# One operand product per group, elementwise work off GpSimd, and projections split 9, 8, 7 in the second MLP of an attention kernel

## The chip, the core and the metric

The kernel runs on one core of a Trainium2 chip. TensorE (PE) multiplies matrices into PSUM; VectorE (DVE), ScalarE (ACT) and GpSimd (POOL) do elementwise work; SyncE (SP) issues every DMA. Each engine works through its own list of instructions strictly in order and waits for others by semaphores. The metric is device time in microseconds (us): 1600.27 us, the median of three runs (1599.98 to 1604.18).

## The reference

Three stages follow each other. A packed attention (8 batches, 8 heads, 576 positions, width 64) makes `x`, 4608 tokens of width 512. Then come two MLPs of width 2048 without biases:

```
h = x @ w_in;   x = (h * (1 / (1 + exp(-h)))) @ w_out      # first MLP
h = x @ w_in2;  out = (h * cos(h)) @ w_out2                # second MLP
```

Everything is float32; the MLP weights come as 64-bit floats, which the kernel decodes itself.

## The kernel before

A float32 product is made of three matmuls on pairs: a number is held as a rounded part and a rest, and rest by rounded, rounded by rest and rounded by rounded are summed in PSUM. `split` makes such a pair: one copy that rounds, one subtraction that leaves the rest.

**Two stages.** From about 0 to 800 us the attention and the first MLP run interleaved. Then comes the second MLP. Its 4608 tokens are cut into nine blocks of 2 x 256 tokens (`NBLK`), and for each block eight groups (`FH`) each take two of the sixteen 128-wide slices of the hidden layer: 72 groups in all.

**A group.** The first matrix product of a group (two token halves, two hidden slices, width 512 in two halves) is done as a 2 x 2 block product with seven products instead of eight. `multiply(s, k)` issues them in four parts, k = 0 to 3: products 0 and 1; 2 and 3; 4 and 5; 6. Between the parts the sums in PSUM are folded: after part 0 ScalarE copies `x1` into `hb` and `x2` into `gf`; after part 1 VectorE adds (`sb<-hb,gf` or `mb<-hb,gf`); after part 2 VectorE adds `hb<-hb,gf`. Part 2 of the products can't start before the first of these adds is done, and part 3 not before the second. In a profile a group is 42 matmuls of 256 columns (into `hb`, `mb`, `sb`) and 24 of 512 columns (into `acc`). `cosine` (ScalarE and VectorE, tiles `n`, `r`, `g`) follows parts 2 and 3, and `project`, two groups later, multiplies by `w_out2` into the four `acc` banks. `second(s)` sets the order: part 0, 12 projections, part 1, 6 projections, part 2, 6 projections, part 3.

**The operands of a block.** `load_y(i)` brings eight tiles `raw` (128 x 256) of the first MLP's output. Where the block holds tokens of the first pair of batches, three more partial sums (`ypart`) come for each tile through two buffers (`ysb`) and are added: 24 adds for blocks 3 and 4, 24 of 64 columns for block 5, none for the others. `put(prod)`, seven times, forms the operand pairs of one product for both halves of the width: up to two subtractions and two splits, into tiles that the profile calls `y`, `w` or `g` by the memory they use. Subtractions go through `combine`, which lets the planner choose VectorE or GpSimd; the rounding copies of `split` may be on ScalarE or VectorE.

**What sets the order.** Nothing is issued as the code stands. Every operation is recorded in a `Plan` with a cost; a list scheduler (`schedule`, `order`) then lists the instructions of all engines, eight rounds forward and backward over the whole kernel, and keeps the round with the earliest planned end. `plan.due` gives the latest times to aim at; in the second MLP a group is due every 10.48 us. From `plan.inorder = []` on, TensorE's operations keep the order of the code. The dependencies recorded in `record` decide the listing only: what an instruction waits for on the chip follows from the tiles it reads and writes. Since all are issued at one place, the profile gives one line (L207) to nearly all instructions, so they are told apart by their tiles.

Of the kernel before, what the change touches and what calls it, by code (L numbers as in the profile page):

```python
# [34 lines left out]
def f32(ap):  # L35

    return ap.bitcast(F32)


class Late:  # L40
# [3 lines left out]
    def __init__(self, key, ap, base=None, path=()):  # L44
        self.key, self.ap, self.base, self.path = key, ap, base or self, path
        if base is None:
            self.tile = None
# [32 lines left out]
class Plan:  # L80
# [21 lines left out]
    def __init__(self, nc):  # L102
        self.ops = []
        self.writes, self.reads = {}, {}
        self.due = None
        self.release = 0.0
        self.margin = 0
        self.inorder = None
        self.block = None
        self.choice = None  # L110
        self.V = self.Engine(self, self.DVE, nc.vector)
        self.A = self.Engine(self, self.ACT, nc.scalar)
        self.T = self.Engine(self, self.PE, nc.tensor)
        self.G = self.Engine(self, self.POOL, nc.gpsimd)
        self.D = self.Engine(self, self.DMA, nc.sync)
# [106 lines left out]
    def record(self, engine, emit, outs, ins, cost, issue):  # L222
        if self.block:
            op = self.ops[-1]
            assert op.engine == engine
            op.emit.append(emit)
            op.cost += cost
        else:
            op = Op()
            op.engine, op.emit, op.cost, op.issue, op.due = engine, [emit], cost, issue, self.due  # L230
            if self.block is not None:
                op.cost += self.TURN
            op.after, op.before, op.choice, op.sbuf = [], [], {}, False
            op.release = self.release
            op.margin = self.margin
            self.ops.append(op)
            if self.block is not None:
                self.block = True
        i = len(self.ops) - 1
        waits = set()  # L240
        if engine == self.PE and self.inorder is not None:
            waits.update(self.inorder)
            self.inorder = [i]
        for r in filter(None, ins):
            if r[1] is None:

                waits.update(
                    j
                    for _, j in self.reads.get(r[0], [])
                    if self.ops[j].engine != engine or self.ops[j].choice or self.choice is not None  # L250
                )
            waits.update(j for s, j in self.writes.get(r[0], []) if self.overlap(s, r[1]))
        for r in filter(None, outs):
            for d in (self.writes, self.reads):
                waits.update(j for s, j in d.get(r[0], []) if self.overlap(s, r[1]))
        for r in filter(None, outs):
            for d in (self.writes, self.reads):
                d[r[0]] = [(s, j) for s, j in d.get(r[0], []) if not self.covers(r[1], s)]
            self.writes[r[0]].append((r[1], i))
        for r in filter(None, ins):  # L260
            self.reads.setdefault(r[0], []).append((r[1], i))
        self.wait(op, i, waits)
# [140 lines left out]
def attention_mlps_kernel(  # L403
# [17 lines left out]
    P = 128  # L421
# [4 lines left out]
    FC = DFF // P  # L426
    KC = DM // P
    TB = 256
    NBLK = NT // (2 * TB)
    FH = FC // 2  # L430
# [4 lines left out]
    plan = Plan(nc)  # L435
# [4 lines left out]
    V, A, T, G, DMA = plan.V, plan.A, plan.T, plan.G, plan.D  # L440
# [43 lines left out]
    acc = [psum.tile([P, 512], F32, name=f"acc{i}") for i in range(4)]  # L484
# [18 lines left out]
    def change(stack, pools, name, side, new):  # L503


        def f():
            stack.close()
            pl = ctx.enter_context(pool(name, side, reuse_waits="tile"))
            for x in new:
                x.tile = pl.tile(list(x.ap.shape), x.ap.dtype, name=x.key)  # L510

        plan.switch(f, sum([cells[pl] for pl in pools], []), [x.key for x in new])
# [15 lines left out]
            V.tensor_copy(dst, src)  # L528

    def combine(dst, x, y, op):  # L530
        with plan.either():
            V.tensor_tensor(dst, x, y, op)
            G.tensor_tensor(dst, x, y, op)

    def split(d, x):

        copy(d[:, 0], x)
        combine(d[:, 1], x, f32(d[:, 0]), ALU.subtract)
# [399 lines left out]
    NS2 = NBLK * FH  # L938
    order = list(range(3, 6)) + [0, 1, 2] + list(range(6, NBLK))
    wout = {}  # L940
# [23 lines left out]
    def load_y(i):  # L964

        t0 = order[i] * TB
        n = min(TB, S - t0)

        def load(kc, h):
            st = raw()  # L970
            DMA.dma_start(st, ydram[kc, :, h * NT // 2 + t0 : h * NT // 2 + t0 + TB])
            for part in ypart if n > 0 else ():
                ad = yad()
                DMA.dma_start(ad[:, :n], part[kc, :, h * S + t0 : h * S + t0 + n])
                combine(st[:, :n], st[:, :n], ad[:, :n], ALU.add)
            return st

        b11 = [load(c, 0) for c in range(2)]
        b12 = [load(c, 1) for c in range(2)]
        b21 = [load(c + 2, 0) for c in range(2)]  # L980
        b22 = [load(c + 2, 1) for c in range(2)]
        t2 = [raw() for c in range(2)]

        def put(prod):
            for c in range(2):
                x, minus = {
                    0: (b11, None),
                    1: (b11, (b12, b11)),
                    2: (t2, (b22, b11)),
                    3: (b21, None),  # L990
                    4: (b12, (b22, b12)),
                    5: (b22, None),
                    6: (b21, (b21, t2)),
                }[prod]
                if minus:
                    combine(x[c], minus[0][c], minus[1][c], ALU.subtract)
                yt[i, prod, c] = yring()
                split(yt[i, prod, c], x[c])

        for prod in range(7):  # L1000
            put(prod)

    def load_wout2(c, w):
        wout[c] = w
        DMA.dma_start(f32(w), w2dram[c])
# [18 lines left out]
    def output(i, t):  # L1024

        o = oring()
        if t % 2:
            V.tensor_scalar(o, acc[t], WEIGHT**-2, None, op0=ALU.mult)
        else:
            A.activation(o, acc[t], AF.Copy, scale=WEIGHT**-2)  # L1030
        p0 = order[i] * TB + t % 2 * P
        cuts = [p0] + list(range(p0 // HALF * HALF + HALF, p0 + P, HALF)) + [p0 + P]
        for a, b in zip(cuts, cuts[1:]):
            r0 = a // HALF * S + t // 2 * HALF + a % HALF
            DMA.dma_start(out[r0 : r0 + b - a, :], o[a - p0 : b - p0])

    gt, st, m5s = {}, {}, {}

    def project(s, x, part):

        if not 0 <= s < NS2:
            return
        i, fp = divmod(s, FH)
        fc = fp + x * FH
        g, w = gt[s, x], wout[fc]
        if fc == FC - 1:
            passes = [(t, a, b) for t in range(4) for a, b in ((1, 0), (0, 1), (0, 0))]
        else:
            passes = [(t, 0, b) for b in (1, 0) for t in range(4)] + [(t, 1, 0) for t in range(4)]
        for n, (t, a, b) in list(enumerate(passes))[6 * part : 6 * part + 6]:  # L1050
            first = fc == 0 and n < 4
            last = fc == FC - 1 and n % 3 == 2
            T.matmul(acc[t], g[:, a, t * P : (t + 1) * P], w[:, b], start=first, stop=last)
            if last:
                output(i, t)

# [34 lines left out]
    def second(s):  # L1091

        plan.due = due_second(s)
        if s == 1:
            for k in range(4):
                for x in range(2):
                    multiply(x, k)
        elif s > 1:
            multiply(s, 0)
            project(s - 2, 0, 0)  # L1100
            project(s - 2, 0, 1)
            multiply(s, 1)
            project(s - 2, 1, 0)
            multiply(s, 2)
            project(s - 2, 1, 1)
            multiply(s, 3)
        plan.due = None

# [5 lines left out]
    def due_second(s):  # L1114
        return due_first(NS) + 10480 * s
# [70 lines left out]
    for pr in range(NPAIR):  # L1186
# [14 lines left out]
        for o in range(PAIR[pr + 1] - PAIR[pr]):  # L1201
# [7 lines left out]
            x = o - 48  # L1209
# [4 lines left out]

    change(top, [att], "yp", "right", raws + ys)
    change(mid, [a2p], "cp", "left", ns + rs_ + g2s + os_)
    load_y(0)
    plan.inorder = []
    for s in range(NS2 + 2):
        i, fp = divmod(s, FH)  # L1220
        if i == 0:
            for x in range(2):
                load_wout2(fp + x * FH, W[2 * fp + x])
        if fp == 0 and i + 1 < NBLK:
            load_y(i + 1)
        second(s)

    with tc.manual_schedule():
# [26 lines left out]
```

## Time and profile before

| | |
|---|---|
| median of 3 runs | 1600.27 us |
| profiled execution | 1597.47 us, span 1595.7 us |
| PE busy | 1544.8 us, 97% of the span |
| DVE busy | 1150.4 us, 72% |
| ACT busy | 780.6 us, 49% |
| POOL busy | 270.3 us, 17% |
| second MLP | about 800 us to the end |

A row of windows gives, for a stretch, the busy time and the count of instructions of each engine, TensorE's granted clock as a share, the busy share of the DMA engines and GB/s. A row of the timeline gives start, duration, engine, line, operation, tiles (out<-in), shapes, and in brackets the idle time before it and what ended it.

### The profile page before, as it was taken

The page shows a single profiled execution, that of the slowest core. Times are in us where ns is not written, and L with a number is a line of the kernel's source. Part 1 is how long each engine was busy: PE and PEld are TensorE (multiplying, and loading weights), DVE is VectorE, ACT ScalarE, POOL GpSimd, SP SyncE. Part 2 cuts the span into 40 slices and gives each one's busy share as a digit, 9 for nine tenths or more (in the row PEclk, how much of TensorE's full clock was granted, in tenths as well). Part 3 has the DMA queues.
Part 4 walks back from the last instruction along what each step waited for, and adds up shares of the span by engine and source line. Part 5 has one row for each costly group of instructions (what it writes and reads, how often), then busy time and mean ns, then how long its engine had stood idle before and what let it go on. Part 6 is the DMA issues. An engine that isn't in the chain of part 4 may idle for free.

```text
span 1595.7 us, 31482 instructions
## 1 busy us (share of the span) xinstructions
PE 1544.8 (97%) x11640; PEld 1384.5 (87%) x11640; DVE 1150.4 (72%) x2140; ACT 780.6 (49%) x1663; POOL 270.3 (17%) x294
## 2 busy tenths in 40 slices
PE   9989999999999999999999999999999999999999
PEld 7778888999789997999988888889898888889997
DVE  5897656465788768787578778776767677686665
ACT  5875544344555655555344444444444444443443
POOL 0230101010322214122212122131202011020000
PEclk9799999999999999999999999999999999999999
DMA  9566374122776777554876867666565656555561
GB/s 269 186 223 184 99 164 124 54 46 58 179 226 177 194 188 217 172 191 144 270 248 185 263 189 249 199 193 209 183 199 173 211 168 215 175 169 190 176 199 43
DMA packets 304857, 287.30 MB, mean 180 GB/s; under 512 B 166464, under 2 KB 215104, under 8 KB 304704
## 3 DMA queue, kind: packets, MB, share of 16 engines
q1 hardware_dynamic: 304704, 285.30, 59.9%
q8 instruction: 92, 1.51, 0.4%
q14 instruction: 61, 0.50, 0.1%
HBM read 232.00 MB, written 53.22 MB: 179 GB/s over the span
## 4 chain that ended last, share of the span: by engine, by line
PE 72%; DVE 17%; DMA 4%; ACT 2%; issue 2%; SPq 1%; POOL 0%; DVEq 0%; ACTq 0%; POOLq 0%
PE acc L207 38%; PE hb L207 18%; PE sb L207 8%; PE mb L207 8%; DVE r L207 5%; DVE g L207 2%; DVE w L207 2%; DVE wy L207 1%; DVE raw L207 1%; DVE wd L207 1%; SPq L207 1%; DMA wd<-in_moe_w_in 1%; DMA wd<-in_moe_w_out 1%; DVE gf L207 1%; ACT g L207 1%
## 5 line engine op out<-in xcount | busy, mean ns | idle before, releaser
L207 PE MATMUL acc<-g,w 128*128 128x288 f32 x3072 | 475.9, 297 | 5.9 <-ACT ysb L207 3.6
L207 PEld LDWEIGHTS acc<-g,w 128*128 128x128 f32 x3072 | 426.8, 188 | 36.6 <-issue 21.3
L207 PE MATMUL acc<-w,g 128*128 128x512 f32 x1728 | 434.9, 394 | 0.2 <-ACT ysb L207 0.2
L207 PEld LDWEIGHTS acc<-w,g 128*128 128x128 f32 x1728 | 313.6, 190 | 56.4 <-ACT ysb L207 0.7
L207 PE MATMUL hb<-a,w 128*128 128x288 f32 x1536 | 271.8, 304 | 10.9 <-DVE gf L207 4.3
L207 PEld LDWEIGHTS hb<-a,w 128*128 128x128 f32 x1536 | 226.6, 191 | 29.1 <-issue 8.7
L207 POOL TENSOR_TENSOR g<-gf,g 128x288 fp32r<-128x288 f32 x105 | 99.7, 951 | 510.6 <-PE acc L207 269.0
L207 DVE SCALAR_TENSOR_TENSOR gf<-gf,hb 128x288 f32<-128x288 f32 x256 | 111.9, 447 | 74.9 <-ACT gf L207 73.8
L207 ACT CAST g<-gf 128x288 fp32r<-128x288 f32 x236 | 101.9, 433 | 119.0 <-PE acc L207 80.6
L207 ACT ACTIVATE gf<-hb 128x288 f32<-128x288 f32 x256 | 103.0, 410 | 116.2 <-PE hb L207 87.8
L207 DVE TENSOR_TENSOR g<-r,g 128x512 fp32r<-128x512 f32 x138 | 101.1, 733 | 45.9 <-ACT g L207 45.9
L207 PEld LDWEIGHTS hb<-w,w 128*128 128x128 f32 x729 | 104.6, 193 | 22.2 <-DVE sb L207 9.8
L207 ACT ACTIVATE r<-r,half_pi 128x512 f32<-128x512 f32 x144 | 103.7, 721 | 40.7 <-DVE r L207 40.7
L207 PE MATMUL hb<-w,w 128*128 128x256 f32 x729 | 113.5, 287 | 10.0 <-DVE sb L207 7.8
L207 DVE TENSOR_TENSOR g<-gf,g 128x288 fp32r<-128x288 f32 x151 | 71.8, 476 | 69.1 <-PE acc L207 43.1
L207 ACT CAST g<-r 128x512 fp32r<-128x512 f32 x142 | 88.2, 621 | 60.3 <-DVE r L207 60.2
L207 DVE SCALAR_TENSOR_TENSOR r<-n,r 128x512 f32<-128x512 int32 x144 | 103.0, 716 | 2.8
L207 ACT ACTIVATE n<-hb 128x512 int32<-128x512 f32 x72 | 43.1, 598 | 88.7 <-DVE r L207 79.4
L207 DVE TENSOR_TENSOR hb<-hb,gf 128x256 f32<-128x256 f32 x72 | 31.0, 431 | 68.6 <-PE hb L207 68.4
L207 ACT ACTIVATE n<-mb 128x512 int32<-128x512 f32 x36 | 21.5, 598 | 109.3 <-PE mb L207 109.3
L207 PEld LDWEIGHTS hb<-y,w 128*128 128x128 f32 x360 | 53.4, 191 | 24.3 <-DVE sb L207 13.1
L207 PE MATMUL hb<-y,w 128*128 128x256 f32 x360 | 58.2, 287 | 14.6 <-DVE sb L207 10.9
(221 smaller groups left out, 2199.8 us busy)
## 6 DMA issues: line engine op xcount, KB each, us to landing
w<-w2s SPq DMA_DIRECT2D x504, 256.0 KB, 3.6
w2s<-wd SPq DMA_DIRECT2D x28, 512.0 KB, 3.7
wd<-in_moe_w_in SPq DMA_DIRECT2D x24, 512.0 KB, 5.0
w<-w1dram SPq DMA_DIRECT2D x48, 256.0 KB, 3.0
wd<-in_moe_w_out SPq DMA_DIRECT2D x20, 512.0 KB, 4.5
ydram<-ysb SPq DMA_DIRECT2D x64, 144.0 KB, 2.6
raw<-ydram SPq DMA_DIRECT2D x72, 128.0 KB, 3.2
w2dram<-wd SPq DMA_DIRECT2D x16, 512.0 KB, 3.0
```

The source lines that it names most:

```text
L207: run = lambda: emit(*[real(x) for x in args], **{k: real(x) for k, x in kw.items()})
```

## The change

Three things. `load_y` no longer calls `put` seven times but returns it; for block 0 all seven are recorded at once as before, for each later block the loop records the loads at group 0 of the block before and `put(0)` to `put(6)` at its groups 1 to 7. A `gate` (the last TensorE operation recorded so far) is added as a dependency to every operation of another engine that is recorded so. And once `inorder` is on, `combine` is VectorE's alone. Besides, `project` takes a range of the 24 projections instead of halves: 9 after part 0, 8 after part 1, 7 after part 2.

```
+        if engine != self.PE:
+            waits.update(self.gate)
...
     def combine(dst, x, y, op):
+        if plan.inorder is not None:
+            V.tensor_tensor(dst, x, y, op)
+            return
         with plan.either():
...
-        for prod in range(7):
-            put(prod)
+        return put
...
             multiply(s, 0)
-            project(s - 2, 0, 0)
-            project(s - 2, 0, 1)
+            project(s - 2, 0, 9)
             multiply(s, 1)
-            project(s - 2, 1, 0)
+            project(s - 2, 9, 17)
             multiply(s, 2)
-            project(s - 2, 1, 1)
+            project(s - 2, 17, 24)
             multiply(s, 3)
...
-    load_y(0)
+    put = load_y(0)
+    for prod in range(7):
+        put(prod)
     plan.inorder = []
...
+        plan.gate = plan.inorder
         if fp == 0 and i + 1 < NBLK:
-            load_y(i + 1)
+            put = load_y(i + 1)
+        elif i + 1 < NBLK:
+            put(fp - 1)
+        plan.gate = []
         second(s)
```

The listing shows what moves. First VectorE in the last group of a block (here the sixth), up to the add that part 2 of the next group's products waits for (`sb<-hb`); `raw` and `w` belong to the next block's operands. Before:

```order
L207 TENSOR_TENSOR raw_8362<-raw_8364,raw_8362 128x256
L207 TENSOR_SCALAR r_8917<-r_8917 128x512
L207 TENSOR_TENSOR g_8920<-r_8916,g_8920 128x512
L207 TENSOR_TENSOR w_1141<-raw_8361,w_1141 128x256
L207 TENSOR_TENSOR raw_8369<-raw_8367,raw_8361 128x256
L207 TENSOR_TENSOR r_8917<-r_8917,hb_92 128x512
L207 TENSOR_TENSOR raw_8364<-raw_8368,raw_8364 128x256
L207 CAST w_1149<-raw_8365 128x256
L207 TENSOR_TENSOR w_1149<-raw_8370,w_1149 128x256
L207 TENSOR_TENSOR sb<-hb_93,gf_149 128x256
L207 TENSOR_TENSOR g_8921<-r_8917,g_8921 128x512
L207 TENSOR_TENSOR raw_8365<-raw_8365,raw_8369 128x256
```

The same place in the changed kernel:

```order
L208 TENSOR_TENSOR raw_8514<-raw_8514,raw_8518 128x256
L208 TENSOR_TENSOR raw_8515<-raw_8515,raw_8519 128x256
L208 SCALAR_TENSOR_TENSOR r_8854<-n_8852,hb_92 128x512
L208 TENSOR_TENSOR r_8853<-r_8853,mb 128x512
L208 SCALAR_TENSOR_TENSOR r_8854<-n_8852,r_8854 128x512
L208 TENSOR_TENSOR w_101<-raw_8514,w_101 128x256
L208 TENSOR_SCALAR r_8854<-r_8854 128x512
L208 TENSOR_TENSOR g_8857<-r_8853,g_8857 128x512
L208 TENSOR_TENSOR w_1142<-raw_8515,w_1142 128x256
L208 TENSOR_TENSOR r_8854<-r_8854,hb_92 128x512
L208 TENSOR_TENSOR sb<-hb_93,gf_149 128x256
L208 TENSOR_TENSOR g_8858<-r_8854,g_8858 128x512
```

One product's four subtractions are left here, and the add now stands ahead of the second `g`; the work of the other products stands in the six groups before.

Next TensorE between parts 1 and 2 of a group (`mb` and `hb` are products, `acc` projections). Before:

```order
L207 MATMUL mb<-y_8378,w_1146 128x256 x3
L207 MATMUL acc_88<-w_1833,g_8921 128x512
L207 MATMUL acc_89<-w_1833,g_8921 128x512
L207 MATMUL acc_90<-w_1833,g_8921 128x512
L207 MATMUL acc_91<-w_1833,g_8921 128x512
L207 MATMUL acc_88<-w_1833,g_8921 128x512
L207 MATMUL acc_89<-w_1833,g_8921 128x512
L207 MATMUL hb_92<-y_8379,w_1146 128x256 x3
```

And now:

```order
L208 MATMUL mb<-y_8527,w_1150 128x256 x3
L208 MATMUL acc_89<-w_1854,g_8857 128x512
L208 MATMUL acc_90<-w_1854,g_8857 128x512
L208 MATMUL acc_91<-w_1854,g_8857 128x512
L208 MATMUL acc_88<-w_1855,g_8858 128x512
L208 MATMUL acc_89<-w_1855,g_8858 128x512
L208 MATMUL acc_90<-w_1855,g_8858 128x512
L208 MATMUL acc_91<-w_1855,g_8858 128x512
L208 MATMUL acc_88<-w_1855,g_8858 128x512
L208 MATMUL hb_92<-y_8528,w_1150 128x256 x3
```

Eight projections instead of six stand between the product that the add reads and the one that waits for the add.

Last VectorE in the second group of block 2, where the partial sums of block 3 (`raw<-raw,ysb`) are added. Before:

```order
L207 TENSOR_TENSOR raw_8362<-raw_8362,ysb_153 128x256
L207 TENSOR_TENSOR raw_8362<-raw_8362,ysb_154 128x256
L207 TENSOR_TENSOR hb_92<-hb_92,gf_148 128x256
L207 SCALAR_TENSOR_TENSOR r_8916<-n_8914,mb 128x512
L207 SCALAR_TENSOR_TENSOR r_8916<-n_8914,r_8916 128x512
L207 TENSOR_SCALAR r_8916<-r_8916 128x512
L207 SCALAR_TENSOR_TENSOR r_8917<-n_8915,hb_92 128x512
```

And now:

```order
L208 TENSOR_TENSOR raw_8510<-raw_8510,ysb_153 128x256
L208 TENSOR_TENSOR raw_8510<-raw_8510,ysb_154 128x256
L208 TENSOR_TENSOR hb_92<-hb_92,gf_149 128x256
L208 SCALAR_TENSOR_TENSOR r_8853<-n_8851,mb 128x512
L208 SCALAR_TENSOR_TENSOR r_8853<-n_8851,r_8853 128x512
L208 TENSOR_SCALAR r_8853<-r_8853 128x512
L208 TENSOR_TENSOR raw_8510<-raw_8510,ysb_153 128x256
L208 CAST w_1144<-raw_8510 128x256
L208 SCALAR_TENSOR_TENSOR r_8854<-n_8852,hb_92 128x512
L208 TENSOR_TENSOR r_8853<-r_8853,mb 128x512
L208 SCALAR_TENSOR_TENSOR r_8854<-n_8852,r_8854 128x512
L208 TENSOR_TENSOR raw_8511<-raw_8511,ysb_154 128x256
```

Adds that GpSimd took in between are VectorE's now, in the middle of its cosine work. Since the planner lists the whole kernel, instructions of the first 800 us change places here and there too, with the same counts on TensorE.

## Rows read from the trace of the kernel before

**Rows 1.** The page: shares of the span by engine in the chain that ended last.

```profile
PE 72%; DVE 17%; DMA 4%; ACT 2%; issue 2%; SPq 1%; POOL 0%; DVEq 0%; ACTq 0%; POOLq 0%
```

**Rows 2.** Windows: first stage in two, then the second MLP in three.

```profile
0.00:100.00 100.00, 90.06 (x1057) 72.07 (x1058) 75.44 (x150) 69.32 (x146) 16.87 (x20) 0.88 0.76 225
100.00:817.00 717.00, 703.28 (x5984) 640.65 (x5983) 510.14 (x1016) 372.19 (x873) 144.44 (x141) 1.00 0.58 162
817.00:872.90 55.90, 53.27 (x333) 47.56 (x332) 41.29 (x72) 24.89 (x50) 10.05 (x11) 1.00 0.64 207
872.90:1411.80 538.90, 518.43 (x3170) 463.27 (x3170) 403.65 (x698) 237.43 (x457) 98.23 (x121) 0.98 0.64 200
1411.80:1580.70 168.90, 168.68 (x1059) 152.19 (x1058) 113.59 (x199) 72.41 (x133) 0.74 (x1) 1.00 0.52 164
```

**Rows 3.** Waits of PE, 817 to 1580.7 us: total, times, longest.

```profile
PE hb L207 <- DVE sb L207: 18.7, 9, 2.5
PE hb L207 <- DVE mb L207: 4.2, 7, 1.3
```

**Rows 4.** Window of one stall's end and the time after it.

```profile
1317.60:1320.90 3.30, 3.05 (x13) 3.05 (x14) 3.15 (x7) 1.24 (x4) 2.78 (x4) 0.52 0.43 140
```

**Rows 5.** Timeline of that block's last group, ahead of the stall.

```profile
1310.74 1.19 POOL L207 TENSOR_TENSOR raw<-raw,raw 128x256 f32<-128x256 f32 x1
1311.25 0.96 DVE L207 TENSOR_TENSOR raw<-raw,raw 128x256 f32<-128x256 f32 x1
...
1315.97 0.41 DVE L207 TENSOR_TENSOR raw<-raw,raw 128x256 f32<-128x256 f32 x1
...
1317.38 0.42 DVE L207 TENSOR_TENSOR sb<-hb,gf 128x256 f32<-128x256 f32 x1
...
1317.85 1.65 PE L207 MATMUL hb<-w,w 128*128 128x256 f32 x6 [2.49 <-DVE sb L207]
```

**Rows 6.** Timeline of a group without operand work.

```profile
1274.09 0.43 DVE L207 TENSOR_TENSOR hb<-hb,gf 128x256 f32<-128x256 f32 x1 [1.46 <-PE hb L207]
...
1276.69 1.58 PE L207 MATMUL mb<-w,w 128*128 128x256 f32 x12
...
1276.94 0.43 DVE L207 TENSOR_SCALAR r<-r 128x512 f32<-128x512 f32 x1
...
1278.11 2.91 PE L207 MATMUL acc<-w,g 128*128 128x512 f32 x12
...
1278.58 0.38 ACT L207 COPY gf<-mb 128x256 f32<-128x256 f32 x1
...
1282.10 0.69 DVE L207 TENSOR_TENSOR g<-r,g 128x512 fp32r<-128x512 f32 x1 [0.69 <-ACT g L207]
...
1282.29 1.55 PE L207 MATMUL acc<-w,g 128*128 128x512 f32 x6
...
1282.70 0.42 DVE L207 TENSOR_TENSOR mb<-hb,gf 128x256 f32<-128x256 f32 x1
...
1283.68 0.88 PE L207 MATMUL hb<-w,w 128*128 128x256 f32 x6
```

**Rows 7.** Tile ysb, 850 to 1300 us: durations in ns (min/median/max), waits, landing.

```profile
L207 SPq DMA_DIRECT2D ysb<-ypart x70: 319/320/1227, 871.7 to 1101.2; - x70
L207 POOL TENSOR_TENSOR raw<-raw,ysb x45: 318/727/1278, 871.7 to 1105.5; 128x64 f32<-128x64 f32 x23, 128x256 f32<-128x256 f32 x22
L207 DVE TENSOR_TENSOR raw<-raw,ysb x27: 407/418/426, 871.2 to 1053.2; 128x256 f32<-128x256 f32 x26, 128x64 f32<-128x64 f32 x1
...
  DMA ysb<-ypart: 99.8, 34
...
DMA to landing us min/median/max: 1.7/3.3/5.1
```

**Rows 8.** DVE on the operands: its waits for ypart; one operation's durations.

```profile
DVE raw L207 <- DMA ysb<-ypart: 1.1, 2, 0.9
...
L207 DVE TENSOR_TENSOR raw<-raw,raw x35: 410/954/961, 862.2 to 1408.3; 128x256 f32<-128x256 f32 x35
```

More of the change, by code (lines that the diff above doesn't have):

```diff
@@ L108, in __init__ @@
         self.inorder = None
+        self.gate = []
         self.block = None
@@ L1037, in attention_mlps_kernel, with project @@
     gt, st, m5s = {}, {}, {}
-    def project(s, x, part):
-        if not 0 <= s < NS2:
+    def project(s, a, b):
+        if s < 0:
             return
         i, fp = divmod(s, FH)
[L1044 to L1051, printed above, removed]
+        passes = []
+        for x in range(2):
+            fc = fp + x * FH
+            if fc == FC - 1:
+                passes += [(x, t, j, k) for t in range(4) for j, k in ((1, 0), (0, 1), (0, 0))]
+            else:
+                passes += [(x, t, 0, k) for k in (1, 0) for t in range(4)] + [(x, t, 1, 0) for t in range(4)]
+        for n in range(a, b):
+            x, t, j, k = passes[n]
+            fc = fp + x * FH
             last = fc == FC - 1 and n % 3 == 2
-            T.matmul(acc[t], g[:, a, t * P : (t + 1) * P], w[:, b], start=first, stop=last)
+            T.matmul(acc[t], gt[s, x][:, j, t * P : (t + 1) * P], wout[fc][:, k], start=fc == 0 and n < 4, stop=last)
             if last:
```

## The prediction

> **What bounds the kernel now.** I read the chain of waits first: TensorE holds 72% of it and VectorE 17% [rows 1], so the question is where TensorE waits for VectorE. Then I cut the span into windows [rows 2]. The changed operand work lies between 817 and 1411.8 us, where blocks 1 to 8 are prepared; from 1411.8 to 1580.7 us only products, cosine and projections are left. That last window is the measure of a second MLP without operand work: 1059 matmuls in 168.9 us, 0.1595 us each, TensorE busy for 168.68 us. (A few records may be missing; all three windows are taken to miss alike.) The 333 + 3170 matmuls of the two windows before would take 558.7 us at that rate. They take 55.9 + 538.9 = 594.8 us. So 36.1 us are lost, and that is all that operand work can give back there.
>
> The waits say to whom: TensorE stands still for 18.7 + 4.2 = 22.9 us before matmuls into `hb`, each time for a VectorE add into `sb` or `mb` [rows 3], with 2.5 us the longest. Behind such a wait the granted clock reads 0.52 for 3.3 us, against 1.00 in the quiet window [rows 2, 4]: 1.2 instead of 2.4 GHz, some 1.6 us of work lost each time. The mean of 0.98 over 538.9 us makes 10.8 us. 22.9 + 10.8 = 33.7; the remaining 2.4 us I take for the refilling of the pipeline after each wait.
>
> The timeline shows why the add is late [rows 5]. In the last group of a block a string of `raw` and `w` operations stands before it on VectorE, and beside GpSimd's work such an operation takes 0.96 us (1311.25) where it takes 0.41 otherwise (1315.97). The add starts at 1317.38 and TensorE has waited 2.49 us. Over the stage the median of this subtraction is 954 ns, its minimum 410 [rows 8].
>
> **The change, part by part.**
> *One product per group.* In a group with a product that needs both kinds of work, VectorE gets two subtractions and two rests, 4 x 0.41 = 1.6 us, and at most two casts. In a quiet group the add that part 2 waits for runs at 1282.70, behind a `g` of 0.69 us, and ends at 1283.12; part 2 starts at 1283.68 [rows 6]: 0.56 us to spare. The listing now puts the add ahead of that `g`, which gives back 0.6 us. VectorE also waited 0.69 us for ScalarE ahead of that `g`, room that the new work fills. So 1.6 us of work meet some 0.56 + 0.6 + 0.69 = 1.85 us of room: no wait on TensorE, and no burst in the last group. I cost this at minus 36.1 us, with the clock falls gone because the waits before them are. If 0.5 us of wait stayed in each of the 56 groups that get a product, 28 of the 36.1 us would stay.
>
> *Elementwise work off GpSimd.* It has 11 + 121 + 1 = 133 instructions in the three windows [rows 2], and all go to VectorE. VectorE is busy 113.59 of 168.9 us in the quiet window, 56.8 us per block of 84.45. A block's 22 subtractions and rests add 9.0 us at 0.41, four casts at most 1.2 at 0.29 (my estimate from half the size of the 0.41 row, rounded up): 67.0 us, 79%. The three blocks that prepare blocks 3 to 5 also get 24 adds, at 0.418 us [rows 7] 10.0 us: 77.0 us, 91%, 7.4 us free. No block is full, and what ran beside GpSimd at 0.96 us runs at 0.41. [...]
>
> *Waits for the partial sums.* An add stands in VectorE's in-order list, so if its `ypart` load has not landed, cosine work and the next fold add queue behind it, and TensorE behind those. Before, 98.7 of the 99.8 us of such waits fell on GpSimd (32 times), which nobody waited for, and 1.1 us on VectorE in its 27 adds [rows 7, 8]. How it goes with all 72 on VectorE is not in the trace. Bounds: VectorE's own rate, 1.1 / 27 x 72 = 2.9 us, and GpSimd's, 98.7 / 45 x 72 = 158 us. The listing leaves between two adds on one buffer, where it is tightest, the other add, the fold add, two cosine operations and a clamp. In the quiet group this is from 1274.09 to 1276.94 + 0.43, 3.28 us, plus the other add, 3.6 us in all [rows 6]; issue and landing need 0.32 + 3.3 [rows 7]. They just meet, so I stay near VectorE's row: some 10 us of waits, of which the 3 x 7.4 = 22 us of free time in these blocks takes most. I put 2 us on TensorE.
> The Trainium skill, "DMA: Bandwidth & Descriptors", section "Anatomy of one DMA", fits 2.0 us plus bytes over 436 GB/s per transfer, on another queue than this one's; for 128 KB that is 2.3 us (an estimate), and no add would wait. The trace's median of 3.3 us decides, and by the page the sum would be 2 us lower.
>
> *The gate.* It enters the planner's lists only. Nothing on the chip waits for it, SP's list is only reordered, and it costs 0.
>
> *9, 8, 7.* Twelve projections from 1278.11 and six from 1282.29 to 1283.68 go at 0.23 us each. Part 1 comes 3 x 0.23 = 0.7 us earlier, at about 1280.2; ScalarE's last copy for it ends at 1278.96 [rows 6], so 1.2 us remain. Part 2 comes 0.23 us earlier and part 3 where it was. With no wait in quiet groups, this gains nothing there: 0, and I bound it at plus or minus 4 us (0.06 us over 72 groups).
>
> *The first 817 us.* The planner lists everything anew. TensorE is idle for 9.94 + 13.72 = 23.7 us there [rows 2]. That is the most that could be gained; as much again is my bound for a loss. Counts and structure stay, so I take 0, with plus or minus 6 us as the likely part.
>
> **Sum.** Against the profiled execution: 1597.47 - 36.1 + 2 = 1563.4 us. That execution lies 2.8 us under the median of the runs shown, so against the median: 1600.27 - 34.1 = 1566 us.
>
> **Rivals.**
> *Add loads that half hide.* If each of the 72 adds holds VectorE for 0.6 us, 43 us minus the 22 free leave 21 on TensorE: 1585 us. For it speaks the landing time of up to 5.1 us; against it that VectorE hardly waited in 27 adds.
> *Add loads that hold VectorE, slower.* The same three blocks at GpSimd's rate, 158 - 22 = 136 us minus the 36 gained, make 1700 us. It is slower than before from (36.1 + 22) / 72 = 0.8 us per add on; at 1.0 us, 1614 us. For it: GpSimd did wait 2.2 us per add. Against: GpSimd had nothing else to do, while VectorE has 3.6 us of other work between two loads.
> *The new listing of the first stage costs.* Fifteen more us of idle TensorE there, against 23.7 now, make 1581 us. Only a loss over 34 us would turn the sign.
> *The burst becomes a drip: the change doesn't do what it says.* If the spread work delays the fold add by 0.6 us in each of the 56 groups, 34 us come back and the time stays at 1600 us. Against: the room of 1.85 us above.
>
> **How the numbers follow.** Forecast 0.80; half-hidden loads 0.08; first stage 0.06; drip 0.03; slower by loads 0.03. The forecast's own range: 1600.27 - 36.1 - 7 = 1557 (first stage better) to 1575. To leave out no more than 2 in 10, the upper end goes to 1582, which takes in the first-stage rival and much of the half-hidden loads. 0.3% is 5 us, about what a measurement of this kernel can tell from no change. Faster by more: 0.80 + 0.08 + 0.06 - 0.01 = 0.93; within it: the drip, 0.03; slower: 0.03 + 0.01 for a first stage that goes badly wrong, 0.04.
>
> **What would show it.** Right: from about 817 us every group takes 10.5 us; TensorE's waits for VectorE into `hb` fall from 22.9 us to under 4; the granted clock reads 1.00 in every window there; `raw<-raw,raw` has a median near 0.41 us; VectorE's busy share is near 79%, and near 91% in the blocks with adds. Wrong: waits of VectorE for `ysb<-ypart` beyond 25 us; clock falls at block ends; a wait in every group of the eight; or a second MLP that begins more than 6 us later or earlier than at 817 us.

## The result and the profile after

| | before | after |
|---|---|---|
| median, 4 runs each | 1600.12 us (1597.72 to 1604.18) | 1563.98 us (1561.91 to 1565.72) |
| ratio, 95% interval | | 0.977 [0.975, 0.979] |
| profiled execution | 1597.47 us, span 1595.7 us | 1561.91 us, span 1560.1 us |
| second MLP, fourth group to the last product | 763.7 us | 726.2 us |

The change is faster by 36 us; 1566 was forecast, in a range of 1557 to 1582. The second MLP is counted from the start of its fourth group (819.0 us now, 817.0 before) and ends with the last product into `hb`. It became 37.5 us shorter, begins 2.0 us later, and the tail behind it is as long as before: -37.5 + 2.0 = -35.5 us between the two profiled executions.

The chain of waits of the changed kernel's page, which answers to [rows 1]:

```profile
PE 85%; DVE 8%; DMA 3%; ACT 2%; issue 1%; SPq 0%; POOL 0%; DVEq 0%; ACTq 0%; POOLq 0%
```

VectorE's share fell from 17 to 8%. The windows of the changed kernel, cut at the same marks of the program as [rows 2] (us, then busy us and instructions of PE, PEld, DVE, ACT, POOL, granted clock, DMA share, GB/s):

```profile
100.00:819.00 719.00, 702.46 (x5974) 642.42 (x5974) 504.49 (x1001) 370.23 (x864) 139.46 (x139) 1.00 0.57 159
819.00:871.70 52.70, 52.70 (x332) 47.68 (x332) 39.84 (x81) 23.36 (x46) 0.00 (x0) 1.00 0.71 228
871.70:1376.80 505.10, 505.10 (x3170) 456.85 (x3170) 399.10 (x821) 234.57 (x452) 0.00 (x0) 1.00 0.69 214
1376.80:1545.20 168.40, 168.40 (x1059) 152.32 (x1058) 119.75 (x225) 74.37 (x140) 0.00 (x0) 1.00 0.54 172
```

In the last three rows PE's busy time equals the length of the window, and the clock is 1.00: TensorE waits for nothing. The middle one is 33.8 us shorter than the same 3170 matmuls were. Read VectorE's column too: over the second MLP it has 39.84 + 399.10 + 119.75 = 558.7 us in 1125 instructions, where [rows 2] give 41.29 + 403.65 + 113.59 = 558.5 us in 966 (one that crosses a mark is counted once). VectorE took over 133 instructions of GpSimd's (and some of block 1's), and its busy time is the same. So its old ones had been slow.

No wait of PE is listed from 819 to 1545.2 us; [rows 3] had 22.9 us. VectorE's waits for the partial sums, its subtractions, and the tile `ysb` answer to [rows 7, 8]:

```profile
DVE raw L208 <- DMA ysb<-ypart: 5.3, 10, 1.1
```

```profile
L208 DVE TENSOR_TENSOR raw<-raw,raw x62: 416/418/426, 819.3 to 1451.0; 128x256 f32<-128x256 f32 x62
```

```profile
L208 DVE TENSOR_TENSOR raw<-raw,ysb x72: 217/418/427, 962.0 to 1180.9; 128x256 f32<-128x256 f32 x48, 128x64 f32<-128x64 f32 x24
its engine sat idle before it (us, times) until:
  DMA ysb<-ypart: 5.3, 10
...
DMA to landing us min/median/max: 1.9/3.6/4.9
```

The subtraction has one duration, 416 to 426 ns, where its median was 954. All 72 adds on VectorE wait 5.3 us together, and TensorE behind them not at all. The timeline of a block's last group in the changed kernel answers to [rows 5]:

```profile
1284.79 0.42 DVE L208 TENSOR_TENSOR w<-raw,w 128x256 fp32r<-128x256 f32 x1
...
1286.07 0.42 DVE L208 TENSOR_TENSOR w<-raw,w 128x256 fp32r<-128x256 f32 x1
...
1286.88 2.00 PE L208 MATMUL acc<-w,g 128*128 128x512 f32 x8
1287.08 0.43 DVE L208 TENSOR_TENSOR sb<-hb,gf 128x256 f32<-128x256 f32 x1
...
1288.72 0.88 PE L208 MATMUL hb<-w,w 128*128 128x256 f32 x6
```

The fold add `sb` ends at 1287.51, 1.2 us before the next part starts at 1288.72, and that part follows the eight projections without a gap.

### The profile page after: what moved, and what is told of

Read it like the earlier page. It is cut to its first block, busy times and chain, and to the rows that moved or that the text cites. A ratio compares the mean times of both kernels' runs of the same rounds, so it can differ in the third digit from the quotient of the medians.

```text
span 1560.1 us, 31304 instructions
## 1 busy us (share of the span) xinstructions
PE 1528.3 (98%) x11640; PEld 1376.7 (88%) x11640; DVE 1147.5 (74%) x2285; ACT 775.9 (50%) x1651; POOL 158.8 (10%) x161
## 4 chain that ended last, share of the span: by engine, by line
PE 85%; DVE 8%; DMA 3%; ACT 2%; issue 1%; SPq 0%; POOL 0%; DVEq 0%; ACTq 0%; POOLq 0%
PE acc L208 46%; PE hb L208 20%; PE sb L208 10%; PE mb L208 10%; DVE wy L208 1%; DVE wd L208 1%; DMA wd<-in_moe_w_in 1%; DVE big L208 1%; DVE gf L208 1%; DMA ypart<-ysb 1%; DVE w L208 1%; DMA kin<-in_q 0%; DVE rsb L208 0%; DVE g L208 0%; ACT wd L208 0%
## 5 line engine op out<-in xcount | busy, mean ns | idle before, releaser
L208 PE MATMUL hb<-a,w 128*128 128x288 f32 x1536 | 266.6, 301 | 10.3 <-DVE gf L208 5.7
L208 ACT CAST g<-gf 128x288 fp32r<-128x288 f32 x222 | 95.5, 433 | 110.8 <-PE acc L208 69.6
L208 PE MATMUL hb<-w,w 128*128 128x256 f32 x729 | 110.0, 282 | 0.0
L208 DVE SCALAR_TENSOR_TENSOR r<-n,r 128x512 f32<-128x512 int32 x144 | 99.1, 688 | 2.2
L208 PE MATMUL mb<-w,w 128*128 128x256 f32 x456 | 65.6, 282 | 0.0
L208 PE MATMUL sb<-w,w 128*128 128x256 f32 x444 | 64.1, 282 | 0.0
```

Of the source, the lines that this page charges most:

```text
L208: run = lambda: emit(*[real(x) for x in args], **{k: real(x) for k, x in kw.items()})
```

## The experiments

**What each part gives alone.** The change has three parts: spreading the products over the groups behind a gate (S), VectorE alone (V), and projections as 9, 8, 7 (P). Theory A, the prediction's, credits the gain to S: the burst in a block's last group makes the fold add late. Theory B credits it to V: GpSimd's work beside VectorE makes VectorE slow. Theory C credits it to P: six projections are too short a cover for the add. Single parts and pairs tell them apart.

S alone (`combine` may choose GpSimd again, projections 12, 6, 6):

```
     def combine(dst, x, y, op):
-        if plan.inorder is not None:
-            V.tensor_tensor(dst, x, y, op)
-            return
...
-            project(s - 2, 0, 9)
+            project(s - 2, 0, 12)
```

> One product per group behind the gate, but GpSimd may still take subtractions and the projections stay 12, 6, 6. Theory A (the burst of a block's operand work ahead of one fold add is what costs): nearly all of the gain is here, 1562 to 1572 us, and no clock fall after 860 us. Theory B (what costs is that VectorE operations take 0.96 us beside GpSimd): at least half of the 36 us stays, 1580 to 1600 us, with waits of TensorE for VectorE of 8 to 20 us. Theory C (the cover of six projections is what is too short): 1590 us or more.

V alone (projections 12, 6, 6; all seven products recorded at the loads, no gate):

```
-        plan.gate = plan.inorder
...
-        elif i + 1 < NBLK:
-            put(fp - 1)
+            for prod in range(7):
+                put(prod)
```

> The operand work as before (all seven products free to be listed at once, 12, 6, 6), but its elementwise work on VectorE and ScalarE alone. Theory A: the burst stays, now some 22 operations of 0.41 us on one engine, so a TensorE wait and a clock fall per block stay: 1585 to 1605 us. Theory B: the operations fall from 0.96 to 0.41 us and most of the loss goes: 1563 to 1575 us. Theory C: about 1600 us.

P alone (both edits to `combine` and the loop together, projections left at 9, 8, 7):

> The kernel before with the projections as 9, 8, 7 and nothing else. Theories A and B: within 5 us of before, 1595 to 1603 us; a wait of 2.5 us is not covered by two more projections of 0.23 us. Theory C: 1585 us or less.

S and V (only the three `project` ranges go back to 12, 6, 6):

> The changed kernel with the projections back at 12, 6, 6. Theories A and B: within 5 us of the changed kernel, 1560 to 1569 us, with TensorE waits of under 2 us in the second MLP. Theory C: waits of some 0.2 us return in many groups, 1575 us or more.

S and P (only `combine` goes back):

> The changed kernel, but GpSimd may take subtractions again. Theory A: within 5 us of the changed kernel, 1560 to 1570 us, since one product's work fits in a group either way, although subtractions beside GpSimd take up to 0.96 us. Theory B: 1580 us or more.

V and P (only the loop goes back, as for V alone), so the burst is allowed:

> The changed kernel with the operands of a block free to be listed at once and no gate; VectorE alone and 9, 8, 7 stay. Theory A: a wait and a clock fall per block, 1580 to 1600 us. Theory B: 1563 to 1575 us. It should come out as the kernel without the gate does if the gate is what spreads the work.

Measured, with the second MLP's length in the profile (the expectations call its first group the third):

| parts | median us | ratio to before, 95% interval | second MLP us | less than 763.7 by |
|---|---|---|---|---|
| S | 1582.32 | 0.991 [0.989, 0.994] | 746.4 | 17.3 |
| V | 1567.92 | 0.981 [0.979, 0.984] | 732.8 | 30.9 |
| P | 1588.88 | 0.995 [0.994, 0.997] | 755.2 | 8.5 |
| S, V | 1564.17 | 0.979 [0.977, 0.981] | 728.6 | 35.1 |
| S, P | 1569.91 | 0.982 [0.979, 0.985] | 737.8 | 25.9 |
| V, P | 1560.79 | 0.976 [0.974, 0.978] | 726.9 | 36.8 |
| S, V, P | 1563.98 | 0.977 [0.975, 0.979] | 726.2 | 37.5 |

The profiled execution of S and P was the slowest of its four (1574.5 us, the others 1564.7 to 1570.1), so its 25.9 may be up to some 5 us low.

Theory A falls. S alone gives under half, V alone over four fifths, and beside V and P the spreading adds 0.7 us. Theory C falls too: without P the gain is 35.1 us. Theory B has the largest part but not all: it expected P alone to change the time by less than 5 us, and S and P, which keep GpSimd, to take 1580 us or more; measured are 8 us less and 1569.91 us. The single gains add up to 56.7 us: each part covers some of what the others remove.

The burst itself is still there without S. The operand instructions (those on `raw`) in the last group of block 5, of VectorE, ScalarE and GpSimd, first in the kernel before, then in V alone:

```profile
1308.20:1322.90 14.70, 7.61 (x12) 3.56 (x10) 10.14 (x11) 0.88 0.47 154
```

```profile
1287.80:1298.30 10.50, 5.08 (x14) 3.13 (x9) 0.00 (x0) 1.00 0.59 183
```

VectorE has two instructions more in the burst than before, with the same six projections as cover, and the group takes 10.5 us instead of 14.7. The timeline of V and P at the end of the block:

```profile
1286.38 0.43 DVE L208 TENSOR_TENSOR sb<-hb,gf 128x256 f32<-128x256 f32 x1
...
1287.92 0.88 PE L208 MATMUL hb<-w,w 128*128 128x256 f32 x6
1287.99 0.42 DVE L208 TENSOR_TENSOR w<-raw,w 128x256 fp32r<-128x256 f32 x1
1288.33 0.76 DVE L208 TENSOR_TENSOR raw<-raw,raw 128x256 f32<-128x256 f32 x2
...
1289.33 1.43 DVE L208 TENSOR_TENSOR w<-raw,w 128x256 fp32r<-128x256 f32 x4
```

Seven operand operations run in 2.8 us, each at some 0.4 us, and no matmul waits; in this listing they stand behind the `sb` add. And what S does while GpSimd is allowed, in the timeline of S alone:

```profile
1321.32 1.95 POOL L208 TENSOR_TENSOR raw<-raw,raw 128x256 f32<-128x256 f32 x2
1321.83 0.85 DVE L208 TENSOR_SCALAR r<-r 128x512 f32<-128x512 f32 x1
1322.60 1.23 DVE L208 TENSOR_TENSOR g<-r,g 128x512 fp32r<-128x512 f32 x1
...
1325.72 0.43 DVE L208 TENSOR_TENSOR sb<-hb,gf 128x256 f32<-128x256 f32 x1
...
1326.20 0.62 PE L208 MATMUL hb<-y,w 128*128 128x256 f32 x3 [0.23 <-DVE sb L208]
```

The `g` that takes 0.69 us elsewhere takes 1.23 beside GpSimd, the fold add comes late, and six of a block's eight groups (blocks 5 to 7) take 10.8 to 11.0 us where quiet ones take 10.5. That is the drip of the rivals, at some 0.4 us in such a group. With 9, 8, 7 beside it (S and P) the drip is gone, though GpSimd is still allowed: all groups outside blocks 2 to 4, where the partial sums are added, take 10.5 us.

**The gate.** S, V and P without the gate's line:

```
-        plan.gate = plan.inorder
```

> The changed kernel without the gate: each product is recorded at its group, but the planner is free to list it earlier. Theory A with the planner as the cause of the burst (it lists operand work as soon as the tiles of the block before last come free, which is in one group): the burst comes back, 1580 to 1600 us, with clock falls at block ends. Rival (that the products are recorded group by group is enough): 1560 to 1569 us.

Measured: 1560.59 us, ratio 0.976 [0.974, 0.978], second MLP 727.7 us. The burst is back: in the trace the four engines run the same operations on the same tiles in the same order as in V and P. So the gate is what spreads the work, recording the products group by group does nothing without it, and this is V and P a second time (727.7 and 726.9 us; 1560.59 and 1560.79 in all). The time came out as the rival expected, but not for its reason. Against the kernel with the gate the second MLP is 1.5 us longer and the whole 3.4 us shorter, and the intervals of the two ratios overlap. The gate gives nothing here.

**One buffer for the partial sums.** This tries the term for the add waits, which the prediction took as its most dangerous one.

```
-    yad = ring([t[:, :TB] for t in ysb_tiles])
+    yad = ring([t[:, :TB] for t in ysb_tiles[:1]])
```

> The changed kernel with one buffer instead of two for the partial sums, so that each add must wait for a load issued after the add before it. If the two buffers just cover the landing (3.6 us of other work against 0.32 + 3.3 us), one does not: VectorE waits more than 25 us for the partial sums, TensorE waits more than 5 us in the blocks with adds, 1570 to 1600 us. Rival (the planner spreads the adds so widely that the landing never counts): within 5 us of the changed kernel.

Measured: 1585.39 us, 0.992 [0.990, 0.994] of before; the second MLP takes 749.9 us, 23.7 more than with two. VectorE's waits for `ysb` came to 13.4 us only, in 18 times, where more than 25 were expected. The loss is elsewhere, in TensorE's waits and in the clock, which reads 0.50 for 10.2 us from within each of the two long ones (1045.9 and 1141.5 us):

```profile
PE hb L208 <- ACT w L208: 8.2, 2, 7.4
PE hb L208 <- ACT y L208: 7.9, 1, 7.9
```

The listing spread the adds so widely that 54 of 72 found their load landed, and the chain of 24 loads then ran past the end of the block: the adds for block 3 last until 1049.2 us, the block starts at 1037.6, and the first groups of blocks 3 and 4 take 22.5 and 21.7 us. So loads can cost as much as feared, by a chain that misses its block and not by many small waits.

**GpSimd's interference by itself.** The pairs change which engine does what and the listing at once. To separate these, I took V alone and gave GpSimd work whose result nobody uses: for each operand pair one addition of two halves of it into a spare tile. The instructions of TensorE and VectorE and their order are unchanged.

```
+                if plan.inorder is not None:
+                    spare = [t.rearrange("p j n -> p (j n)") for t in pbds]
+                    G.tensor_tensor(spare[0], f32(yt[i, prod, c][:, 0]), f32(yt[i, prod, c][:, 1]), ALU.add)
+                    plan.ops[-1].cost = 0
```

> The kernel with only the elementwise work moved to VectorE (1567.9 us, all seven products free to be listed at once, 12, 6, 6), plus 112 additions on GpSimd whose result nobody uses: each reads one finished operand pair of 128 x 256 and writes a spare tile, 14 a block. VectorE's and TensorE's lists are the same, instruction for instruction. Theory B (VectorE is slowed by GpSimd's reading beside it): the subtractions rise from 0.42 to up to 0.96 us, a wait per block comes back, 1578 to 1600 us. Rival D (time was lost before because VectorE's list waited for GpSimd's results): nobody waits for these, so 1563 to 1572 us.

As control, the same number of unused copies on ScalarE (`A.copy(spare[0], f32(yt[i, prod, c][:, 1]))`):

> The same with the 112 extra operations as copies on ScalarE instead (some 0.40 us each), as a control: theory B, within 5 us of the kernel without them, 1563 to 1573 us, since VectorE's durations stay; if any extra work that hangs on the operands costs time, as much as with GpSimd.

Measured: with idle GpSimd work 1598.79 us, ratio to before 1.000 [0.999, 1.002]: the whole gain of V is gone. With idle ScalarE work 1567.0 us, 0.980 [0.977, 0.983], as V alone. The second MLP in one window: V alone, with GpSimd's idle work, with ScalarE's (columns as above):

```profile
818.20:1551.00 732.80, 728.54 (x4556) 655.87 (x4555) 547.59 (x1078) 340.26 (x659) 0.00 (x0) 1.00 0.64 201
```

```profile
817.00:1582.40 765.40, 739.48 (x4556) 657.78 (x4556) 583.03 (x1078) 341.74 (x659) 76.37 (x98) 0.99 0.61 192
```

```profile
814.40:1547.00 732.60, 728.54 (x4556) 655.55 (x4556) 548.17 (x1078) 370.08 (x757) 0.00 (x0) 1.00 0.63 201
```

98 additions on GpSimd, 76.4 us long, make VectorE's same work 35.4 us longer, and the stage 32.6. 98 copies on ScalarE leave both as they were. Nobody waits for GpSimd; TensorE waits for VectorE again:

```profile
PE hb L208 <- DVE mb L208: 17.9, 9, 2.6
PE hb L208 <- ACT hb L208: 4.9, 7, 1.0
PE hb L208 <- DVE hb L208: 1.7, 6, 0.3
PE hb L208 <- DVE sb L208: 1.1, 2, 0.9
```

The same three operations, in the timeline of V alone and then beside the idle work:

```profile
1296.35 1.08 DVE L208 TENSOR_TENSOR w<-raw,w 128x256 fp32r<-128x256 f32 x3
```

```profile
1318.00 5.90 POOL L208 TENSOR_TENSOR pbd<-w 128x256 f32<-128x256 f32 x6 [2.65 <-DVE w L208]
...
1318.83 2.39 DVE L208 TENSOR_TENSOR w<-raw,w 128x256 fp32r<-128x256 f32 x3
...
1325.60 0.62 PE L208 MATMUL hb<-y,w 128*128 128x256 f32 x3 [0.96 <-ACT hb L208]
```

1.08 us became 2.39. VectorE's groups of instructions under the idle work say which kinds suffer:

```profile
L208 DVE TENSOR_TENSOR g<-r,g 128x512 fp32r<-128x512 f32 x138 | 103.9, 753 | 38.9 <-ACT g L208 38.8
...
L208 DVE TENSOR_TENSOR r<-r,hb 128x512 f32<-128x512 f32 x69 | 47.2, 684 | 6.8 <-ACT r L208 6.7
...
L208 DVE TENSOR_TENSOR w<-raw,w 128x256 fp32r<-128x256 f32 x53 | 28.1, 542 | 0.0
```

In V alone these means are 688, 686 and 418 ns. The Trainium skill, page "SBUF — State Buffer", section "Who interferes with whom", says that a VectorE instruction with two inputs in SBUF contends with a GpSimd instruction that reads SBUF, and that one with at most one such input does not, unless it runs in one of VectorE's 2-port modes. The rows fit as far as they go: `g<-r,g` and `w<-raw,w` grew, `r<-r,hb`, with one input in PSUM, did not. No run here varied the memory of an input by itself.

Operations with a single input in SBUF can grow as well: the clamp `r<-r` of S alone (1321.83 above) took 0.85 us where it takes 0.43 elsewhere, and in the kernel before a rounding cast took 0.81 us where it takes 0.29:

```profile
1316.02 0.95 POOL L207 TENSOR_TENSOR w<-raw,w 128x256 fp32r<-128x256 f32 x1 [0.85 <-ACT w L207]
...
1316.31 0.81 DVE L207 CAST w<-raw 128x256 fp32r<-128x256 f32 x1
```

Whether these ran in such a mode no run shows. In the same rows the durations go with who begins first. The subtraction at 1315.97 [rows 5] began 0.05 us ahead of this GpSimd operation and took 0.41 us. In the second MLP of the kernel before, the operand operations with two inputs of 256 columns (adds included) that began while GpSimd ran had a median of 0.95 us (43 of them); the 22 during which GpSimd began had 0.41.

**VectorE everywhere.** If GpSimd's help costs this in the second MLP, it may in the first stage. V and P, with `combine` VectorE's alone from the start:

```
     def combine(dst, x, y, op):
-        if plan.inorder is not None:
-            V.tensor_tensor(dst, x, y, op)
-            return
-        with plan.either():
-            V.tensor_tensor(dst, x, y, op)
-            G.tensor_tensor(dst, x, y, op)
+        V.tensor_tensor(dst, x, y, op)
```

> VectorE alone for subtractions in the first stage too, on top of VectorE alone and 9, 8, 7 in the second MLP without spreading (1560.8 us). Theory B carried further: the first stage loses its slowed operations as well and ends up to 10 us earlier, 1550 to 1559 us. Rival: some 75 us of work more make VectorE the bound of the first stage, 1565 to 1585 us.

Measured: 1539.16 us, ratio 0.963 [0.960, 0.966], the fastest of all, ahead of both kernels compared here, and earlier than the 1550 to 1559 expected. Its first stage in windows:

```profile
0.00:100.00 100.00, 90.73 (x1145) 73.87 (x1146) 78.94 (x175) 77.62 (x167) 0.70 (x6) 1.00 0.86 238
100.00:795.00 695.00, 688.94 (x5915) 632.67 (x5915) 515.27 (x1119) 367.69 (x856) 0.00 (x0) 1.00 0.57 162
```

The second MLP starts at 791.8 us, 25.7 earlier than in V and P. From its first matmul on TensorE is idle 8.4 us less there (14.0 against 22.4), and the clock never falls, while V and P spend 27.3 us of the first stage at half clock, some 13.6 us of work; the other 3.7 us are not accounted for. Whether less interference does this or the other listing that comes with it was not separated.

**How far a listing moves by itself.** V and P with 24 planner rounds in place of 8:

```
-ROUNDS = 8
+ROUNDS = 24
```

> That same 1560.8 us kernel with 24 planner rounds instead of 8: another listing of the first stage, the second MLP unchanged (727 us from its third group on, within 1). If listings of the first stage differ by some 3 us as those seen so far, 1556 to 1566 us; a gain of more than 5 us would say that the first stage's listing is worth more than the rest of the change.

Measured: 1563.94 us, 0.978 [0.975, 0.980], second MLP 727.2 us as with 8, the first stage 2 us longer. Over the kernels that keep GpSimd in the first stage, the second MLP begins between 814.3 and 820.0 us. Not all of that is the listing: V and P began it at 817.5 us and the same listing without the gate's line at 816.1. Differences of some 3 us between kernels therefore say nothing about an edit.

## Why the prediction was right, and where not

- **The size of the loss: right.** "So 36.1 us are lost, and that is all that operand work can give back there": measured 37.5. The quiet window as a measure of TensorE's rate without waits held: 1059 matmuls take 168.40 us now, with block 8's operands made beside them, 168.90 then, and the busy windows run at that rate.
- **Which part gives it: wrong.** The words "no wait on TensorE, and no burst in the last group. I cost this at minus 36.1 us" stood under the one product per group. Without it, VectorE alone and 9, 8, 7 give 36.8 us with the burst in place; with it alone 17.3 come. The part headed "Elementwise work off GpSimd" named the cause, 0.96 us beside GpSimd and 0.41 otherwise, and had no price of its own: I only asked whether VectorE would be full. (Its row for 0.41, at 1315.97, was no quiet one: GpSimd began 0.05 us later.) The total came out right because the three parts together take all the loss away, whichever of them is credited.
- **The room of 1.85 us in a group: right with GpSimd away, or in blocks without adds.** It was worked out at undisturbed durations. With GpSimd allowed and 12, 6, 6 (S alone), the cosine operations beside the spread work took 0.85 and 1.23 us where 0.43 and 0.69 are usual, and the drip comes. With GpSimd allowed and 9, 8, 7 as in the prediction (S and P) it doesn't: the 11.6 us lost against S, V and P lie in five groups of blocks 2 to 4.
- **9, 8, 7 at nothing: wrong as a term.** I priced it from quiet groups, where nothing is late. Where a fold add is late, three projections fewer behind part 0, two more behind part 1 and one more behind part 2 move the slack to where it is short: 8.5 us alone, 5.9 on top of V, at least 8.6 on top of S, 2.4 on top of both.
- **Waits for the partial sums: mechanism right, size under.** VectorE waited 5.3 us, not some 10, and none reached TensorE, against 2 us. The room between two loads adds up to 3.28 + 0.42 = 3.7 us, not 3.6. The experiment with one buffer shows that the second one carries this.
- **The clock: right.** The falls of the second MLP went with the waits ahead of them. The gate: it sets the listing only, as predicted, and it alone spreads the work; without it the time is no worse.
- **The first 817 us:** 2.0 us later, inside the 6 us allowed.
- **VectorE's share: 84 and 76%, not 91 and 79.** Two blocks, one with adds and one without, in the changed kernel:

```profile
966.30:1050.60 84.30, 84.30 (x530) 76.26 (x530) 70.80 (x147) 40.11 (x78) 0.00 (x0) 1.00 0.78 238
1218.90:1303.00 84.10, 84.10 (x531) 76.06 (x530) 63.58 (x127) 38.39 (x74) 0.00 (x0) 1.00 0.63 201
```

- **A misreading without effect on the sum.** I took the windows from 817 us as holding the operand work of blocks 1 to 8. The operands of block 1 were made before 817 us, and the burst in a block's last group was for the block after the next: tiles come free there, and the list takes up all work that is ready.

## What to carry to other kernels

A second engine that takes work off a busy one is worth its instructions minus what it does to the durations of the first, and both are in the trace: look for one operation with two durations, and for who runs beside the long one. Where several edits are made together, price each from the rows as if it came alone; a sum that fits says nothing about which edit earned it. Suspected interference can be tested by itself with work that nobody uses, on the suspected engine and on another as control, the lists of the others left as they are.

## What the runs showed of the hardware

98 GpSimd additions of 0.78 us, used by nobody, lengthened VectorE's work by 35.4 us, 0.36 us for each, and undid 31 us of a 1568 us kernel. An operation with two inputs of 256 columns went from 0.41 to 0.96 us, one of 512 columns from 0.69 to 1.23, a cast from 0.29 to 0.81. Two-input operations of 256 columns already running when GpSimd began stayed at 0.41. VectorE without help did 159 more instructions in the same 558 us.
